# Attention and feed-forward network on one core: a planner's table of operation lengths and result delays is set anew

## The chip, the cores and the metric

The kernel runs on one core of a Trainium2 chip. The metric is the device time of one execution in microseconds (us); the median of several runs counts. A core has five instruction queues that are followed in order: TensorE (PE, matrix products; PEld is its loading of weights), VectorE (DVE), ScalarE (ACT), GpSimd (POOL) and SyncE (SP, which here issues every DMA). An instruction that waits holds up all that stand behind it in its queue.

## The reference

```python
scores = scale * np.matmul(q, k.transpose(0, 1, 3, 2))       # 8 batches x 8 heads, 576 x 576, depth 64
thresh = np.max(scores, axis=-1, keepdims=True) - tau
scores = np.where(scores >= thresh, scores, -1000000000.0)
attn = np.exp(scores - np.max(scores, axis=-1, keepdims=True))
attn = attn / (np.sum(attn, axis=-1, keepdims=True) + 1e-09)
x = np.matmul(attn, v)                                        # heads side by side: 4608 x 512
r = np.maximum(x @ w_in, 0.0)                                 # 512 x 2048
out = (s * (r * r) + b) @ w_out                               # 2048 x 512
```

`tau` is 0.02. `w_in` and `w_out` come as 64-bit floats, which the kernel turns into 32-bit floats itself.

## The kernel before, in words

**Attention.** A tile is 128 rows of queries of one head against all 576 keys. Batch 0 (36 tiles, "plain") is computed in 32-bit floats: scores on PE (L481), the row's maximum on DVE (L484), the exponential on ACT (L488), threshold and sum on DVE (L490), the division on POOL (L496), transposes on PE (L504), a copy on ACT (L508) and the product with the values on PE (L517). Batches 1 to 7 (252 tiles, "split") use pairs of 16-bit floats, a high and a low part of each number. Such a tile goes through scores on PE (L545, into bank `s` or `t`), maximum on DVE (L549), bias on ACT (L553) and the threshold on POOL (L551), exponential on ACT (L555), threshold and sum on DVE (L557), a small POOL instruction (L560), reciprocal on DVE (L562), high part on ACT (L563), low part on DVE (L566), and then a transposing DMA issued by SP (L571) into the tiles `ea` and `eb`. When the 4 or 5 tiles of a visit are there, PE multiplies them with the values (L581, 28 matmuls); there are 56 such groups. Since the first and the last link of this chain are on PE, it has to be covered by other PE work.

**Weights.** In the first hundred microseconds the 16 slices of `w_in` and the 16 of `w_out` are loaded (L601, L604) and converted: two ACT instructions (L625, L628) and one DVE instruction (L620) for a slice. Then their size is found (L643 to L667), and only after that ACT (L692) and DVE (L696) make the 16-bit pieces that the network's matmuls need.

**Feed-forward network.** The rows of `x` go through in 18 blocks of 256 rows, each in 16 steps, 288 steps in all. A step is 12 matmuls into bank `h` (L794), three ACT instructions (L798 reads `h`, L801 squares, L802 makes the high part `gh`), one on POOL for the low part `gl` (L803; on DVE in the last block), and two groups of three matmuls (L809: two with `gh`, one with `gl`) into bank `o`. Bank `h` counts as one, so the next step's matmuls have to wait until L798 has read it.

**What sets the order.** Nothing runs where the code calls it. Each call of `plan.add` only records an operation with its engine, its keys (what it reads and writes) and two numbers: how long it occupies its engine, and after how long its result is there. `Plan.run` adds to the second number a fixed time for the way to another engine (`HANDOVER`), and `Plan.place` fills every engine's queue with a list scheduler: of the operations whose inputs are there by these numbers, the most urgent goes next. It runs forward and backward four times and keeps the order whose planned end is earliest; then the instructions are issued in that order. On the chip the queues and semaphores alone decide when something runs, so the numbers act only through the order. 76 matmuls with no result (L933, "busy" fillers) stand in places of the first plain tiles.

Of the kernel before, what the change touches and what calls it, by code (L numbers as in the profile page):

```python
# [37 lines left out]
class Plan:  # L38
# [7 lines left out]
    HANDOVER = 150  # L46
# [70 lines left out]
    def run(self):  # L117
# [24 lines left out]
def tile_attention_ffn(ctx: ExitStack, tc: tile.TileContext, qT, kT, v, tau, w_in, w_out, s, b, out):  # L142


    nc = tc.nc
# [103 lines left out]
    def pe(n, cols, fn, r, w, at):  # L249

        plan.add("PE", (n * (0.417 * cols + 3), n * (0.417 * cols + 3) + 170), fn, r, w, at)
# [13 lines left out]
    def dma(kb, fn, r, w, at):  # L265
        plan.add("SP", (max(600, kb * 4.4), 1550 + kb * 4.4), fn, r, w, at)

    def load(kb, fn, r, w, at):
        plan.add("SP", (max(620, kb * 4.4), 1550 + kb * 4.4), fn, r, w, at)


    def transfer(rows, fn, r, w, at):
        plan.add("SP", (1640, 3190), fn, r, w, at)

    class Plain:
# [27 lines left out]
        def load(self, at):  # L303
# [18 lines left out]
            if self.p:  # L322
                act((1900, 2000), zeros, ["qt0", "qt1"], [(self.tag, "z")], at)
# [41 lines left out]
    class Visit:  # L365
# [31 lines left out]
        def prepare(self, at):  # L397
# [5 lines left out]
            for c, (t, keys) in enumerate([(t, [k]) for t, k in raw] + [(flat, kr)]):  # L403
                w = t.shape[-1]
                ks.append((f"vm{m}", c))
                dve((67 + 1.04 * w, 150 + 1.04 * w), lambda c=c, t=t: nc.vector.tensor_reduce(
# [16 lines left out]
            for c, (t, key) in enumerate(raw):  # L423
                up, hi, lo = x[:, 9 + c:10 + c], 1 - c, 2 + c
                act((612, 717), lambda hi=hi, t=t, up=up: nc.scalar.activation(
                    out=self.piece(hi), in_=t, func=AF.Copy, scale=up), [key, (kx, 3)], [self.kpc[hi]], at)
                dve2((658, 743), lambda hi=hi, lo=lo, t=t, up=up: nc.vector.scalar_tensor_tensor(
# [17 lines left out]
            for hd in self.hds:  # L445
# [4 lines left out]
                act((350, 453), lambda hd=hd, own=own, j=j, up=up: nc.scalar.activation(  # L450
                    out=hd.values()[:, :, own], in_=rv[:, j], func=AF.Copy, scale=up), kr + [(kx, 3)], keys, at)
                dve2((400, 485), lambda hd=hd, own=own, other=other, j=j, up=up: nc.vector.scalar_tensor_tensor(
# [15 lines left out]
    def plain_tile(ti, i):  # L468
# [13 lines left out]
        plan.add("PE", (990, 1160), scores, ti.kq(), [bk, ("begun", i)], i - SCORES_AHEAD)  # L482
# [7 lines left out]
        dve((740, 900), lambda: nc.vector.scalar_tensor_tensor(  # L490
# [5 lines left out]
        pool((740, 748), lambda: nc.gpsimd.tensor_scalar(  # L496
# [8 lines left out]
        pe(5, 240, transposes, [em_k, "ident"], ["t"], i + 0.5)  # L505
        ke = ("e32", ti.slot)

        act((690, 790), lambda: nc.scalar.copy(out=e32(ti.slot), in_=tp), ["t"], [ke], i + 0.5)  # L508
        if ti.plain:
# [9 lines left out]
            plan.add("PE", (8.5 * n + 240, 8.5 * n + 410), products, [("e32", slot) for slot, _ in cuts] + [(pr.tag, "z")] + pr.kept[1] + [  # L519
                k for x in pr.keys[2:] for k in (x, x + (1,))], ["pv"], i + VALUES_AFTER)  # L520
            act((80 + 0.75 * n, 180 + 0.75 * n), lambda: nc.scalar.copy(out=dest, in_=bank["pv"][:, 0:n]), ["pv"], keys,
                i + VALUES_AFTER)

    def split_tile(ti, i):
# [21 lines left out]
        plan.add("PE", (4 * 123 + (190 if ti.slot is None else 0), 4 * 123 + (360 if ti.slot is None else 170)), scores,  # L546
# [4 lines left out]
        pool((260, 263), lambda: nc.gpsimd.tensor_scalar(  # L551
            out=line, in0=top, scalar1=-1.0, scalar2=va.wz[:, 2:3], op0=ALU.mult, op1=ALU.add), [(ks_, 0), (va.kwz, 2)], [(ks_, 1)], i - 0.5)
# [4 lines left out]
        dve((740, 900), lambda: nc.vector.scalar_tensor_tensor(  # L557
# [5 lines left out]
        act((668, 774), lambda: nc.scalar.activation(out=pieces[:, 0:S], in_=ex, func=AF.Copy, scale=unit),  # L563
            [em_k, (ks_, 3)], [en_k], i)
        act((142, 242), lambda: nc.scalar.copy(out=pieces[:, S:S + T], in_=pieces[:, 0:T]), [en_k], [(en_k, 1)], i)
# [500 lines left out]
```

## Time and profile before

| | |
|---|---|
| median of 3 runs | 1137.09 us (1134.49 to 1138.08) |
| the profiled execution, its own time | 1137.64 us |
| its span, first to last instruction | 1135.8 us |
| PE busy | 1106.7 us (97%) |
| DVE, ACT, POOL busy | 917.3, 967.7, 546.5 us |
| DMA queues, share of 16 engines | 65% |
| granted TensorE clock | 1.00 of full speed in every slice |

Busy time is the union of an engine's instructions. The length that the profile gives for one instruction runs from start to end; on ACT and DVE the next one starts some 0.1 us before that end, so what an instruction takes of its engine is read from start to start.

### The profile page before, as it was taken

What the parts mean: (1) busy time and instruction counts of PE and PEld (TensorE: products, weight loads), DVE (VectorE), ACT (ScalarE), POOL (GpSimd) and SP (SyncE); (2) the same over time, 40 slices, a digit from 0 to 9 for tenths busy, and PEclk for the clock granted to TensorE, in tenths of its full rate; (3) what the DMA queues carried; (4) which work ended last, traced back from release to release, by engine and by line L of the source; (5) the groups of instructions that cost most, each with busy time, mean ns of one, the idle gap of its engine ahead of it and who ended that gap; (6) DMA issues with size and microseconds to landing.
All of it is one profiled execution on the core that took longest, in us unless ns stands there. A gap on an engine that the chain in (4) does not pass through costs nothing.

```text
span 1135.8 us, 26196 instructions
## 1 busy us (share of the span) xinstructions
PE 1106.7 (97%) x8882; PEld 770.5 (68%) x8882; DVE 917.3 (81%) x1950; ACT 967.7 (85%) x2301; POOL 546.5 (48%) x1117
## 2 busy tenths in 40 slices
PE   8998999999999999999999999999999999999998
PEld 7776656666676666766666667666666667666665
DVE  5898889898999998989789799988988898875021
ACT  7997889889999988999889799998889989896443
POOL 5665445455645554545435355554545555443200
PEclk9999999999999999999999999999999999999999
DMA  8940069777987987668757499777876777563000
GB/s 277 342 143 1 13 163 178 145 151 138 213 151 136 156 195 166 137 117 168 168 113 149 84 179 181 163 142 167 163 153 130 131 152 126 94 110 58 10 20 19
DMA packets 360438, 156.27 MB, mean 138 GB/s; under 512 B 314224, under 2 KB 342384, under 8 KB 360304
## 3 DMA queue, kind: packets, MB, share of 16 engines
q1 hardware_dynamic: 360304, 154.60, 65.1%
q8 instruction: 70, 1.15, 0.4%
q14 instruction: 64, 0.52, 0.2%
HBM read 46.01 MB, written 9.44 MB: 49 GB/s over the span
## 4 chain that ended last, share of the span: by engine, by line
PE 74%; ACT 8%; DVE 6%; issue 3%; DMA 3%; POOL 1%; SPq 1%; DVEq 0%; ACTq 0%; POOLq 0%
PE h L794 27%; PE o L809 27%; PE pv L581 7%; PE s L545 4%; PE t L545 4%; ACT en L563 2%; ACT em L555 1%; DVE em L557 1%; DMA eb<-en 1%; PE pv L517 1%; DVE st L549 1%; ACT iw L798 1%; DMA ea<-en 1%; PE t L504 1%; PE s L481 1%
## 5 line engine op out<-in xcount | busy, mean ns | idle before, releaser
L794 PE MATMUL h<-xp,iw 128*128 128x256 f16 x3456 | 424.8, 273 | 10.2 <-ACT iw L798 9.4
L794 PEld LDWEIGHTS <-iw 128*128 128x128 f16 x3456 | 335.2, 98 | 100.1 <-issue 20.5
L803 POOL TENSOR_TENSOR gl<-iw,gh 128x256 f16<-128x256 f32 x272 | 202.3, 744 | 208.4 <-issue 82.6
L566 DVE SCALAR_TENSOR_TENSOR en<-em,st,en 128x576 f16<-128x576 f32 x252 | 209.6, 836 | 21.4 <-ACT en L563 20.1
L563 ACT ACTIVATE en<-em,st 128x576 f16<-128x576 f32 x252 | 193.0, 768 | 17.0 <-DVE st L562 9.4
L809 PE MATMUL o<-ow,gh 128*128 128x512 f16 x648 | 192.9, 379 | 0.7 <-DVE iw L823 0.7
L551 POOL TENSOR_SCALAR st<-st,wz 128x1 f32<-128x1 f32 x252 | 121.5, 483 | 111.3 <-DVE st L549 68.0
L798 ACT ACTIVATE iw<-h 128x256 f32<-128x256 f32 x288 | 108.0, 375 | 71.2 <-PE h L794 62.8
L809 PEld LDWEIGHTS <-gh 128*128 128x128 f16 x1152 | 108.2, 98 | 77.7 <-issue 8.2
L560 POOL TENSOR_SCALAR st<-st 128x1 f32<-128x1 f32 x252 | 86.1, 342 | 144.1 <-DVE em L557 76.2
L809 PE MATMUL o<-iw,gh 128*128 128x512 f16 x504 | 150.0, 379 | 0.2 <-DVE iw L823 0.2
L809 PE MATMUL o<-ow,gl 128*128 128x512 f16 x324 | 122.8, 379 | 0.0
L801 ACT ACTIVATE iw<-iw 128x256 f32<-128x256 f32 x288 | 119.4, 415 | 3.7
L802 ACT CAST gh<-iw 128x256 f16<-128x256 f32 x288 | 115.5, 401 | 4.5 <-PE o L809 0.5
L557 DVE SCALAR_TENSOR_TENSOR em<-t,st,em 128x576 f32<-128x576 f32 x126 | 102.3, 812 | 19.9 <-ACT em L555 13.6
L545 PEld LDWEIGHTS <-ow 128*128 128x128 f16 (+1 forms) x980 | 85.1, 100 | 47.8 <-issue 13.5
L557 DVE SCALAR_TENSOR_TENSOR em<-s,st,em 128x576 f32<-128x576 f32 x126 | 102.3, 812 | 13.0 <-ACT em L555 8.9
L555 ACT ACTIVATE em<-s,st,wz 128x576 f32<-128x576 f32 x126 | 103.9, 824 | 1.1
L555 ACT ACTIVATE em<-t,st,wz 128x576 f32<-128x576 f32 x126 | 103.8, 824 | 1.1
L553 ACT ACTIVATE st<-st,wz 128x1 f32<-128x1 f32 x252 | 72.9, 290 | 36.3 <-DVE st L549 34.8
L809 PEld LDWEIGHTS <-gl 128*128 128x128 f16 x576 | 56.3, 98 | 68.0
L549 DVE TENSOR_REDUCE st<-t 128x1 f32<-128x576 f32 x126 | 94.4, 749 | 8.8 <-PE t L545 7.2
(198 smaller groups left out, 1836.1 us busy)
## 6 DMA issues: line engine op xcount, KB each, us to landing
ow<-k SPq DMA_DIRECT2D x98, 216.0 KB, 3.5
rk<-in_k_dram SPq DMA_DIRECT2D x29, 288.0 KB, 3.3
iw<-in_moe_w_in_dram SPq DMA_DIRECT2D x16, 512.0 KB, 6.8
ow<-in_moe_w_out_dram SPq DMA_DIRECT2D x16, 512.0 KB, 6.1
out_dram<-iw SPq DMA_DIRECT2D x32, 256.0 KB, 2.5
rq<-in_q_dram SPq DMA_DIRECT2D x28, 288.0 KB, 3.6
rv<-in_v_dram SPq DMA_DIRECT2D x56, 128.0 KB, 2.8
qs<-k SPq DMA_DIRECT2D x14, 216.0 KB, 3.6
```

The costliest lines, as they stand in the source:

```text
L545: nc.tensor.matmul(to, y[:, 0, q], y[:, w, c], start=(w == 1), stop=(w == 2))
L551: pool((260, 263), lambda: nc.gpsimd.tensor_scalar(out=line, in0=top, scalar1=-1.0, scalar2=va.wz[:, 2:3], op0=ALU.mult, op1=ALU.add), [(k ...
L555: act((636, 740), lambda: nc.scalar.activation(out=halves, in_=ps, func=AF.Exp, bias=bias, scale=va.wz[:, 1:2]), [bk, (ks_, 4), (va.kwz, 1 ...
L557: dve((740, 900), lambda: nc.vector.scalar_tensor_tensor(out=halves, in0=ps, scalar=line, in1=halves, op0=ALU.is_ge, op1=ALU.mult, accum_o ...
L563: act((668, 774), lambda: nc.scalar.activation(out=pieces[:, 0:S], in_=ex, func=AF.Copy, scale=unit), [em_k, (ks_, 3)], [en_k], i)
L566: dve2((740, 825), lambda: nc.vector.scalar_tensor_tensor(out=pieces[:, S + T:2 * S + T], in0=ex, scalar=unit, in1=pieces[:, 0:S], op0=ALU ...
L794: nc.tensor.matmul(ps, wi[w][f][:, c * P:(c + 1) * P], x[:, u, c, :], start=(c == 0 and i == 0), stop=(c == NC - 1 and i == 2))
L798: act((357, 473), lambda: nc.scalar.activation(out=g(), in_=ps, func=AF.Relu, scale=H_DOWN), [h, (f"w{SPARES[(0, 1, 5)[k3]]}", "i", 2)], [ ...
L801: act((320, 417), lambda: nc.scalar.activation(out=g(), in_=g(), func=AF.Square), [kg], [kg], at)
L802: act((308, 405), lambda: nc.scalar.copy(out=hi, in_=g()), [kg], [f"gh{k3}"], at)
L803: do((712, 735) if not self.last else (340, 425), lambda: eng.tensor_tensor(out=lo, in0=g(), in1=hi, op=ALU.subtract), [kg, f"gh{k3}"], [f ...
L809: nc.tensor.matmul(bank["o"][:, t, :], a[:, ts_], w, start=(f == 0 and i == 0), stop=(f == NF - 1 and i == 2))
```

## The change

The numbers given to `plan.add` are replaced, and the fixed time for the way to another engine becomes 40 ns, or 110 ns where the receiver is POOL, in place of 150 ns everywhere. No instruction is added, removed or altered; the counts of instructions on each engine are the same. The core of the diff (other lines of the same kind are left out):

```diff
-    HANDOVER = 150
+    HANDOVER, TO_POOL = 40, 110
...
-                lag = p[2] + self.HANDOVER if p[0] != o[0] else p[2] if p[0] != "PE" else p[1]
+                lag = p[2] + (self.TO_POOL if o[0] == "POOL" else self.HANDOVER) if p[0] != o[0] else p[2] if p[0] != "PE" else p[1]
...
     def load(kb, fn, r, w, at):
-        plan.add("SP", (max(620, kb * 4.4), 1550 + kb * 4.4), fn, r, w, at)
+        plan.add("SP", (max(660, kb * 3.5), 2000 + kb * 5), fn, r, w, at)
...
     def transfer(rows, fn, r, w, at):
-        plan.add("SP", (1640, 3190), fn, r, w, at)
+        plan.add("SP", (1450, 3400), fn, r, w, at)
...
-        act((636, 740), lambda: nc.scalar.activation(out=halves, in_=ps, func=AF.Exp, bias=top, scale=1.0),
+        act((633, 800), lambda: nc.scalar.activation(out=halves, in_=ps, func=AF.Exp, bias=top, scale=1.0),
...
-        pool((260, 263), lambda: nc.gpsimd.tensor_scalar(
+        pool((290, 255), lambda: nc.gpsimd.tensor_scalar(
             out=line, in0=top, scalar1=-1.0, scalar2=va.wz[:, 2:3], op0=ALU.mult, op1=ALU.add), [(ks_, 0), (va.kwz, 2)], [(ks_, 1)], i - 0.5)
-        act((100, 200), lambda: nc.scalar.activation(out=bias, in_=top, func=AF.Copy, scale=va.wz[:, 1:2]),
+        act((185, 300), lambda: nc.scalar.activation(out=bias, in_=top, func=AF.Copy, scale=va.wz[:, 1:2]),
             [(ks_, 0), (va.kwz, 1)], [(ks_, 4)], i - 0.5)
-        act((636, 740), lambda: nc.scalar.activation(out=halves, in_=ps, func=AF.Exp, bias=bias, scale=va.wz[:, 1:2]),
+        act((716, 885), lambda: nc.scalar.activation(out=halves, in_=ps, func=AF.Exp, bias=bias, scale=va.wz[:, 1:2]),
...
-            plan.add("PE", (12 * 0.427 * NB, 12 * 0.427 * NB + 170), products, self.kx + [(f"w{f}", "i", 2)], [h], at)
-            act((357, 473), lambda: nc.scalar.activation(out=g(), in_=ps, func=AF.Relu, scale=H_DOWN),
+            plan.add("PE", (12 * 0.4265 * NB, 12 * 0.4265 * NB + 220), products, self.kx + [(f"w{f}", "i", 2)], [h], at)
+            act((264, 400), lambda: nc.scalar.activation(out=g(), in_=ps, func=AF.Relu, scale=H_DOWN),
...
-            do((712, 735) if not self.last else (340, 425), lambda: eng.tensor_tensor(out=lo, in0=g(), in1=hi, op=ALU.subtract),
+            do((735, 735) if not self.last else (400, 490), lambda: eng.tensor_tensor(out=lo, in0=g(), in1=hi, op=ALU.subtract),
```

The first place is ACT's queue at the first plain tiles, from the first exponential on (`em` are the exponentials, `iw` and `ow` slices of the weights, `x` and `rv` the transposed tiles). Before:

```order
L488 ACTIVATE em_78<-s,st_69 128x576
L488 ACTIVATE em_79<-o,st_70 128x576
L488 ACTIVATE em_80<-s,st_71 128x576
L508 COPY x_113<-t 128x640
L488 ACTIVATE em_78<-o,st_72 128x576
L625 ACTIVATE iw_235<-iw_235 128x512
L508 COPY rv<-t 128x640
L628 ACTIVATE iw_235<-iw_235 128x512
```

After:

```order
L488 ACTIVATE em_78<-s,st_69 128x576
L625 ACTIVATE iw_187<-iw_187 128x512
L488 ACTIVATE em_79<-o,st_70 128x576
L628 ACTIVATE iw_187<-iw_187 128x512
L488 ACTIVATE em_80<-s,st_71 128x576
L508 COPY x_113<-t 128x640
L488 ACTIVATE em_78<-o,st_72 128x576
L625 ACTIVATE ow_221<-ow_221 128x512
```

The two conversions of the first slice have moved from behind the fourth exponential to behind the first and the second.

The second place is ACT's queue in the first block of the network, from the reading of bank `h` (L798) in step 13 on, where the first split tiles come in (`k` is a piece of a raw tile, `st` are row statistics, `gh` the high part). Before:

```order
L798 ACTIVATE iw_292<-h 128x256
L425 ACTIVATE k<-rq,vs_103 128x576
L553 ACTIVATE st_71<-st_71,wz_90 128x1
L801 ACTIVATE iw_292<-iw_292 128x256
L555 ACTIVATE em_80<-s,st_71,wz_90 128x576
L553 ACTIVATE st_72<-st_72,wz_90 128x1
L802 CAST gh_115<-iw_292 128x256
L555 ACTIVATE em_78<-t,st_72,wz_90 128x576
L798 ACTIVATE iw_325<-h 128x256
```

After:

```order
L798 ACTIVATE iw_236<-h 128x256
L801 ACTIVATE iw_236<-iw_236 128x256
L802 CAST gh_115<-iw_236 128x256
L798 ACTIVATE iw_285<-h 128x256
L801 ACTIVATE iw_285<-iw_285 128x256
L802 CAST gh_116<-iw_285 128x256
L798 ACTIVATE iw_333<-h 128x256
```

Two exponentials, two biases and a conversion of a raw tile no longer stand between the two readings of `h`; the first split tiles come later, behind 16 steps of the network where it was 12.

## Rows read from the trace of the kernel before

**Rows 1.** The profile's page: span, and each engine's busy time.
```profile
span 1135.8 us, 26196 instructions
PE 1106.7 (97%) x8882; PEld 770.5 (68%) x8882; DVE 917.3 (81%) x1950; ACT 967.7 (85%) x2301; POOL 546.5 (48%) x1117
```

**Rows 2.** Busy time of each engine by stretch of 50 us; then clock, DMA share, GB/s.
```profile
0.00:50.00 50.00, 45.81 (x341) 38.21 (x343) 35.60 (x84) 41.70 (x81) 30.20 (x81) 1.00 0.94 320
50.00:100.00 50.00, 46.20 (x454) 36.21 (x452) 44.61 (x104) 43.15 (x79) 30.07 (x57) 1.00 0.35 113
100.00:150.00 50.00, 47.38 (x381) 33.08 (x380) 38.95 (x72) 44.72 (x93) 26.56 (x44) 1.00 0.14 35
150.00:200.00 50.00, 46.01 (x349) 31.31 (x349) 45.65 (x100) 42.97 (x102) 24.87 (x52) 1.00 0.87 167
200.00:250.00 50.00, 47.31 (x401) 32.91 (x396) 45.50 (x97) 46.12 (x111) 24.84 (x51) 1.00 0.76 147
...
700.00:750.00 50.00, 50.00 (x411) 34.39 (x410) 45.94 (x98) 46.26 (x113) 25.15 (x53) 1.00 0.77 155
...
1100.00:1136.00 36.00, 31.45 (x211) 20.45 (x209) 6.51 (x14) 13.46 (x34) 0.00 (x0) 1.00 0.04 15
```

**Rows 3.** PE's waits in the whole run: us in total, times, longest.
```profile
PE h L794 <- ACT iw L798: 9.4, 9, 1.9
PE s L545 <- DVE em L557: 2.1, 2, 1.5
```

**Rows 4.** Timeline of PE, 155 to 163 us: start, length, instructions [idle before].
```profile
155.63 1.47 PE L794 MATMUL h<-xp,iw 128*128 128x256 f16 x12
158.98 1.47 PE L794 MATMUL h<-xp,iw 128*128 128x256 f16 x12 [1.88 <-ACT iw L798]
...
160.94 0.59 PE L809 MATMUL o<-iw,gh 128*128 128x512 f16 x2
...
161.59 1.47 PE L794 MATMUL h<-xp,iw 128*128 128x256 f16 x12
162.90 0.17 PE L411 MATMUL pv<-vm,onesb 128*128 128x4 bf16 x1
```

**Rows 5.** Timeline of ACT in the same stretch.
```profile
156.15 0.28 ACT L553 ACTIVATE st<-st,wz 128x1 f32<-128x1 f32 x1
...
156.64 0.81 ACT L555 ACTIVATE em<-s,st,wz 128x576 f32<-128x576 f32 x1
157.36 0.28 ACT L553 ACTIVATE st<-st,wz 128x1 f32<-128x1 f32 x1
...
158.56 0.37 ACT L798 ACTIVATE iw<-h 128x256 f32<-128x256 f32 x1
```

**Rows 6.** Timeline of ACT at the first plain tiles, and at 31 us.
```profile
10.62 0.74 ACT L488 ACTIVATE em<-o,st 128x576 f32<-128x576 f32 x1 [0.97 <-DVE st L484]
13.44 0.74 ACT L488 ACTIVATE em<-s,st 128x576 f32<-128x576 f32 x1 [2.08 <-DVE st L484]
...
30.92 0.67 ACT L625 ACTIVATE iw<-iw 128x512 f32<-128x512 f32 x1
31.48 0.68 ACT L628 ACTIVATE ow<-ow 128x512 int32<-128x512 uint16 x1
```

**Rows 7.** ACT's longest wait in 0 to 30 us: total, times, longest.
```profile
ACT em L488 <- DVE st L484: 5.3, 4, 2.1
```

**Rows 8.** As rows 2, around the network's first step.
```profile
100.00:105.00 5.00, 3.74 (x41) 3.00 (x40) 3.82 (x10) 4.70 (x8) 3.23 (x11) 1.00 0.01 2
105.00:110.00 5.00, 3.64 (x29) 3.15 (x29) 4.73 (x11) 5.00 (x12) 4.23 (x5) 1.00 0.01 3
```

**Rows 9.** The transposing DMAs of L571, all 280, from issue to landing.
```profile
DMA to landing us min/median/max: 2.8/3.4/7.0
```

**Rows 10.** POOL's threshold instruction L551: length in ns, min/median/max.
```profile
L551 POOL TENSOR_SCALAR st<-st,wz x252: 255/266/1402, 148.2 to 1025.7; 128x1 f32<-128x1 f32 x126
```

**Rows 11.** The page's group of DVE's low part L566: busy us, mean ns.
```profile
L566 DVE SCALAR_TENSOR_TENSOR en<-em,st,en 128x576 f16<-128x576 f32 x252 | 209.6, 836 | 21.4 <-ACT en L563 20.1
```

More of the change, by code (lines that the diff above doesn't have):

```diff
@@ L249, in pe @@
     def pe(n, cols, fn, r, w, at):
-        plan.add("PE", (n * (0.417 * cols + 3), n * (0.417 * cols + 3) + 170), fn, r, w, at)
+        plan.add("PE", (n * (0.417 * cols + 3), n * (0.417 * cols + 3) + 165), fn, r, w, at)
     def dve(cost, fn, r, w, at, port=False):
@@ L504, in transposes @@
                 nc.tensor.transpose(out=tp[:, t, :], in_=ex[:, c:c + P], identity=ident())
-        pe(5, 240, transposes, [em_k, "ident"], ["t"], i + 0.5)
+        plan.add("PE", (573, 816), transposes, [em_k, "ident"], ["t"], i + 0.5)
         ke = ("e32", ti.slot)
-        act((690, 790), lambda: nc.scalar.copy(out=e32(ti.slot), in_=tp), ["t"], [ke], i + 0.5)
+        act((572, 797), lambda: nc.scalar.copy(out=e32(ti.slot), in_=tp), ["t"], [ke], i + 0.5)
         if ti.plain:
@@ L518, in products @@
                                          e32(slot)[:, kt, cs], start=(kt == 0), stop=(kt == 4))
-            plan.add("PE", (8.5 * n + 240, 8.5 * n + 410), products, [("e32", slot) for slot, _ in cuts] + [(pr.tag, "z")] + pr.kept[1] + [
+            plan.add("PE", (8 * n + 220, 8 * n + 320), products, [("e32", slot) for slot, _ in cuts] + [(pr.tag, "z")] + pr.kept[1] + [
                 k for x in pr.keys[2:] for k in (x, x + (1,))], ["pv"], i + VALUES_AFTER)
-            act((80 + 0.75 * n, 180 + 0.75 * n), lambda: nc.scalar.copy(out=dest, in_=bank["pv"][:, 0:n]), ["pv"], keys,
+            act((50 + 0.83 * n, 150 + 0.83 * n), lambda: nc.scalar.copy(out=dest, in_=bank["pv"][:, 0:n]), ["pv"], keys,
                 i + VALUES_AFTER)
@@ L545, in scores @@
                         nc.tensor.matmul(to, y[:, 0, q], y[:, w, c], start=(w == 1), stop=(w == 2))
-        plan.add("PE", (4 * 123 + (190 if ti.slot is None else 0), 4 * 123 + (360 if ti.slot is None else 170)), scores,
+        plan.add("PE", (490 + (214 if ti.slot is None else 0), 650 + (126 if ti.slot is None else 0)), scores,
                  [("y", 2 * va.n + j, c) for j in js for c in range(2)], [bk], i - SCORES_AHEAD)
@@ L562, in split_tile @@
         dve((73, 157), lambda: nc.vector.reciprocal(out=unit, in_=total), [(ks_, 2)], [(ks_, 3)], i)
-        act((668, 774), lambda: nc.scalar.activation(out=pieces[:, 0:S], in_=ex, func=AF.Copy, scale=unit),
+        act((666, 760), lambda: nc.scalar.activation(out=pieces[:, 0:S], in_=ex, func=AF.Copy, scale=unit),
             [em_k, (ks_, 3)], [en_k], i)
-        act((142, 242), lambda: nc.scalar.copy(out=pieces[:, S:S + T], in_=pieces[:, 0:T]), [en_k], [(en_k, 1)], i)
-        dve2((740, 825), lambda: nc.vector.scalar_tensor_tensor(
+        act((135, 225), lambda: nc.scalar.copy(out=pieces[:, S:S + T], in_=pieces[:, 0:T]), [en_k], [(en_k, 1)], i)
+        dve2((728, 830), lambda: nc.vector.scalar_tensor_tensor(
             out=pieces[:, S + T:2 * S + T], in0=ex, scalar=unit, in1=pieces[:, 0:S], op0=ALU.mult, op1=ALU.subtract),
@@ L582, in products @@
                                      lazy[("ea", "eb")[j]][:, n, g.c0:g.c0 + g.n], start=(i == 0), stop=(i == len(slots) - 1))
-        cost = len(slots) * (0.417 * g.n + 3) + 150
-        plan.add("PE", (cost, cost + 170), products, g.keys + [k for hd in g.hds for k in hd.kvs], ["pv"], at)
+        cost = len(slots) * (0.417 * g.n + 3) + 206
+        plan.add("PE", (cost, cost + 85), products, g.keys + [k for hd in g.hds for k in hd.kvs], ["pv"], at)
         hd = g.hds[0]
@@ L724, in sums @@
         hs = ["h"]
-        plan.add("PE", (8 * 216, 8 * 216 + 170), products, [(f"w{f}", "o", 2) for f in fs] + ["ones16"], hs, at)
+        plan.add("PE", (8 * 216, 8 * 216 + 160), products, [(f"w{f}", "o", 2) for f in fs] + ["ones16"], hs, at)
         if k == 0:
@@ L728, in sums @@
         else:
-            dve((660, 745), lambda: nc.vector.tensor_tensor(out=spare(2), in0=bank["h"], in1=spare(2), op=ALU.add),
+            dve((600, 680), lambda: nc.vector.tensor_tensor(out=spare(2), in0=bank["h"], in1=spare(2), op=ALU.add),
                 hs + ["bias"], ["bias"], at)
@@ L755, in stage @@
             for u, c in enumerate(self.cuts):
-                dve((100 + 4.2 * size[u], 190 + 4.2 * size[u]), lambda u=u, c=c: nc.vector.tensor_reduce(
+                dve((63 + 4.17 * size[u], 143 + 4.17 * size[u]), lambda u=u, c=c: nc.vector.tensor_reduce(
                     out=nm[:, u:u + 1], in_=self.src[:, :, c], axis=mybir.AxisListType.XY, op=ALU.max,
@@ L773, in stage @@
                 up = pw[:, 2, u:u + 1]
-                act((110 + 3.64 * size[u], 212 + 3.64 * size[u]), lambda c=c, up=up: nc.scalar.activation(
+                act((185 + 3.34 * size[u], 285 + 3.34 * size[u]), lambda c=c, up=up: nc.scalar.activation(
                     out=get()[:, 0, :, c], in_=self.src[:, :, c], func=AF.Copy, scale=up),
@@ L777, in stage @@
                     [kx, (kx, 0), (kx, 1)] + [(kx, h, v) for h in range(2) for v in range(4)] if not u else [(kx, 0, u)], at)
-                dve2((130 + 4.18 * size[u], 230 + 4.18 * size[u]), lambda c=c, up=up: nc.vector.scalar_tensor_tensor(
+                dve2((135 + 4.15 * size[u], 225 + 4.15 * size[u]), lambda c=c, up=up: nc.vector.scalar_tensor_tensor(
                     out=get()[:, 1, :, c], in0=self.src[:, :, c], scalar=up, in1=get()[:, 0, :, c], op0=ALU.mult,
```

38 lines of the change are left out of this document (19 added, 19 removed).

## Prediction

> **What bounds the kernel now.** I read the page first: PE is busy for 1106.7 of 1135.8 us [rows 1]. The reader should take two things from it. The same matmuls are issued before and after, so the change can only move the time that PE is not at work, some 29 us, and whatever useless waiting hides inside its busy time. And the other engines have room on average, so they matter only where PE waits for them.
>
> The table by stretches [rows 2] says where the 29 us lie. PE lacks 4.2, 3.8, 2.6, 4.0 and 2.7 us in the first five stretches of 50 us, 17.3 us together. At 700 us it lacks nothing in 50. At the very end it lacks 4.6, which is the last result's way out. So the first 250 us and the end hold 22 of the 29 us; the some 850 us between them hold about 7. The granted clock is 1.00 throughout and is no part of the question.
>
> Then the waits of PE [rows 3]. The largest has one cause: the next step's matmuls (L794) wait until ACT has read bank `h` (L798), 9.4 us in 9 places, the longest 1.9. The next largest is 2.1. The rest of the idle time is start, end and short gaps.
>
> Last the timeline at the longest of these waits [rows 4, 5]. A step occupies PE for 1.31 us (161.59 to 162.90). Here the next step stands directly behind one that began at 155.63, and starts only at 158.98. ACT is why: it was working through biases and exponentials, and came to L798 at 158.56. One such exponential takes ACT 157.36 − 156.64 = 0.72, and a bias (L553) lasts 0.28 from start to end. The old table has 0.636 for the first and lets the second's result be there after 0.200; the new one has 0.716 and 0.300. So the old plan believed that ACT would be through earlier than it can be, and the order that it made puts PE in front of a door that is still shut.
>
> **The change, part by part.** No instruction is added or removed, so each term is a wait that moves.
>
> *Steps that stand close together.* I counted in the two orders how much PE work lies between one step's matmuls and the next's, with 0.65 us for a group of L809 [rows 4] and about 0.5 for a split score tile. Before, 11 places have at most one such group or tile between them, in five of them nothing at all; after, it is 8, in two of them nothing and in one a single small matmul. The 9.4 us lie nearly all at these places [rows 3], 0.85 us for each of the 11. Eight of them at that price are 6.8 us: a gain of 2.6 us. The bounds: with ACT's lengths right, all eight could be free of waits, a gain of 9.4; or each could cost the longest wait, 1.9, which is 15.2 in all and a loss of 5.8. I take the middle price, since the places that stay are of the same kind, the first one again in the first block.
>
> *The start.* In the first 30 us ACT waits four times, 5.3 us together, for the maximum of a plain tile [rows 7]. Into two of these waits (0.97 and 2.08) the new order puts the first slice's two conversions [rows 6], 0.56 us each (30.92 to 31.48). That is 1.1 us that ACT needn't spend later. The whole of the conversions moves forward: the first L692, which needs all of them, stands behind 32 exponentials and 30 copies of plain tiles before, behind 29 and 27 after. So the network's first step should come some 4 to 5 us earlier (six instructions at about the 0.6 that a conversion takes, and the 1.1). This is not a gain of that size: the three tiles' work is still to be done, and PE has then done about as much less by that time. I cost the shift itself at nothing, since ACT is busy 42 to 45 us of each 50 in that part [rows 2] and what it does first it doesn't do later; the cover is the plain tiles left over, which now lie beside the first steps, where PE stands idle for 2.6 us of 10 [rows 8]. If they cover that too, 2.6 more are gained; if the weights land too late for their new places, each late slice stops ACT and the plain tiles behind it, and I allow 4 us of loss for that, half of the 8.0 us that PE lacks in the first 100 us [rows 2]. I take the 1.1 us.
>
> *The way between engines.* 150 ns become 40 (110 to POOL). A split tile's chain from PE to PE goes over nine such ways, one of them to POOL, so the plan brings the last link nearer to the first: up to 8 × 0.11 + 0.04 = 0.92 us, of which the longer table entries (for the transposing DMA 3.40 in place of 3.19) take back a part. Where PE always has other work this is worth nothing, and at 700 us it has [rows 2]: I cost it at nothing. What hides it is PE work between the last score tile of a visit and the product with the values; that cover shrinks, see the first rival.
>
> *SP's queue.* The table allows a transposing DMA 1.45 us of the queue in place of 1.64, and loads come in another order. All were covered (PE's waits show no DMA of weight [rows 3]): nothing.
>
> The sum is −2.6 − 1.1 = −3.7 us on the profiled execution's 1137.6. That execution lies 0.5 above the median of the three runs, 1137.1, which gives **1133.4 us**, 0.33% less. A measurement of this kernel can tell about 0.3%, 3.4 us, from no change, so the forecast lies at that border.
>
> **The rivals.**
>
> *No change to be seen.* PE is full for most of the run; the 17 us of the first stretches come from a start-up that is a chain (load, convert, find the size, make pieces), and the short filler places are only traded for others of the same price. For it: 97% [rows 1]. Against it: the waits for L798 have a cause that the new table mends [rows 5]. Time 1137.
>
> *The ramp gains more.* With true lengths the stretches from 50 to 250 us, which lack 13.1 us, could come halfway to the 0 of the later ones [rows 2]: 6.5 us in place of the 3.7, and the end stays as it is. With 2.6 from the later steps' waits it is 9.1, so 1128. For it: these stretches are where ACT is fullest and wrong lengths hurt most. Against it: the first split tiles stand behind 16 steps where it was 12, so the attention chain comes in later and its first product too.
>
> *Slower: the product with the values waits for its transposes.* Counted in the order by PE's work, the least distance from a visit's last score tile to its product (L581) falls from 11.6 to 9.5 us, and 7 of the 56 visits lie under 12 us where it was 2. The transposing DMAs land after 3.4 us as a rule, but after 7.0 at the worst [rows 9], and the new plan reckons with 3.4 and a handover of 0.04. A DMA that is late by 3.6 then stops PE, and everything in its queue. If each of the seven loses a third of that, 1.2, the loss is 8.4, and with the 3.7 gained the time is 1141.8. It decides from 7.1 us of such waits on, since up to there the time stays within 0.3% of the old one. For it: the distance that shrinks. Against it: of PE's long waits none was of this kind [rows 3], so there was slack to give.
>
> *Slower: POOL's lengths don't hold.* The table gives the threshold instruction one length, 0.255 to its result. The row shows a median of 0.266 and a longest of 1.402 [rows 10], 1.14 more; a DVE instruction of L566 has 0.836 [rows 11]. In some 20 steps the low part's product now stands 2.6 to 2.8 us behind the step's matmuls by PE's work, where it was 3.2 to 3.4; each needs POOL's `gl`. If POOL is late by half of 1.14 in all of these, and nothing covers it, it costs 20 × 0.57 = 11.4, less the 3.7: 1144.8; with half of them covered, 1139.1. The Trainium skill has the rule for such lateness (SBUF — State Buffer, section "SBUF: two separate sides"): DVE and GpSimd share a port pair as an exclusive lock, and whoever comes second waits for the other's whole instruction. The long tail of the row agrees with it; the rule speaks against a fixed length for POOL, though the planner keeps one such port for both engines, before and after.
>
> **How the numbers follow.** The forecast (1131 to 1136) gets 0.40, no change 0.24, the ramp 0.16, the transposes 0.13, POOL 0.07. The border to "faster" is 1133.7: of the forecast's 0.40 some 0.24 lie below it, with the ramp's 0.16 that is 0.40. The other 0.16 of the forecast, nearly all of the no-change case and a part of POOL's make 0.40 for the same. The transposes, the rest of POOL and a start whose weights come late make 0.20 for slower. The range has to take in the ramp at its best (1128 less some 2) and the transposes (1141.8): 1126 to 1142.
>
> **What the profile would show.** If I am right, PE's waits for L798 fall from 9.4 us to about 7, with fewer of them in the first block; ACT's wait for the maxima in the first 30 us falls by about a microsecond; the first step of the network starts at 97 to 100 us; and no wait of PE on a transposing DMA appears. The forecast is wrong if PE's idle time in the stretches after 250 us grows above the 7 us of before (then the handovers were slack that was needed), or if the first 250 us lack clearly more or less than 17 us.

## The result, and the profile after

The changed kernel took **1148.3 us** (median of 4 runs, 1146.8 to 1151.5), the kernel before 1137.2 beside it: 1.0105 of the time, with an interval of 1.0077 to 1.0133. It is 1% slower, and lies above the range that the prediction gave. The page of the changed kernel, its lines that answer to [rows 1]:

```profile
span 1147.2 us, 26153 instructions
PE 1111.1 (97%) x8882; PEld 770.8 (67%) x8882; DVE 917.4 (80%) x1950; ACT 967.0 (84%) x2301; POOL 538.3 (47%) x1117
```

The span grew by 11.4 us. PE's busy time is 4.4 longer and its idle time 7.0 (1147.2 − 1111.1 = 36.1, where it was 29.1). The table by stretches, with the columns of [rows 2], shows where; first of the kernel after:

```profile
0.00:50.00 50.00, 43.40 (x346) 36.87 (x347) 35.78 (x85) 42.91 (x84) 27.67 (x77) 1.00 0.95 320
50.00:100.00 50.00, 47.28 (x449) 37.04 (x448) 46.65 (x106) 44.91 (x83) 33.55 (x67) 1.00 0.33 113
100.00:150.00 50.00, 49.94 (x393) 34.41 (x392) 36.70 (x68) 40.84 (x87) 25.80 (x38) 1.00 0.03 8
150.00:200.00 50.00, 46.73 (x347) 31.21 (x347) 42.86 (x93) 42.27 (x101) 24.37 (x50) 1.00 0.84 197
200.00:250.00 50.00, 47.75 (x398) 32.35 (x395) 48.72 (x108) 47.29 (x116) 26.10 (x54) 1.00 0.74 138
250.00:600.00 350.00, 344.73 (x2797) 236.96 (x2796) 316.22 (x675) 315.32 (x773) 178.55 (x366) 1.00 0.79 159
600.00:1050.00 450.00, 439.92 (x3545) 301.35 (x3543) 372.24 (x780) 389.26 (x956) 208.32 (x441) 1.00 0.71 134
```

The two long stretches of the kernel before:

```profile
250.00:600.00 350.00, 344.73 (x2806) 237.13 (x2805) 315.77 (x675) 314.66 (x773) 178.96 (x364) 1.00 0.76 154
600.00:1050.00 450.00, 448.38 (x3621) 307.97 (x3619) 379.39 (x801) 397.33 (x975) 219.74 (x453) 1.00 0.71 137
```

In the first 250 us PE lacks 14.9 us where it lacked 17.3: the start did gain 2.4. From 250 to 600 its idle time is the same. From 600 to 1050 PE lacks 10.1 where it lacked 1.6, a loss of 8.5; and the way out at the end lacks about 1 more. PE's waits between 600 and 1050 us (total, times, longest) show what is new there. After:

```profile
PE pv L581 <- DMA eb<-en: 3.3, 5, 1.1
PE h L794 <- ACT iw L798: 1.7, 4, 0.6
PE t L545 <- DVE em L557: 1.6, 3, 0.8
PE s L545 <- DVE em L557: 1.5, 1, 1.5
PE pv L581 <- DMA ea<-en: 0.8, 1, 0.8
PE pv L704 <- ACT x L588: 0.4, 1, 0.4
```

Before, the same stretch held 1.3 us of waits in all, none of them longer than 0.4 and none on a DMA:

```profile
PE o L809 <- DVE iw L823: 0.7, 2, 0.4
PE h L794 <- DVE xp L778: 0.2, 1, 0.2
PE h L794 <- ACT iw L798: 0.2, 1, 0.2
PE h L794 <- ACT xp L774: 0.2, 1, 0.2
```

Now products wait for their transposes (4.1 us, six times), scores for a bank, steps for ACT. Over the whole run `h` waits 5.2 us for L798 (9.4 in [rows 3]), L581 4.9 us for the transposing DMAs (none before), and L545 6.9 us (2.8 before), of which 4.6 are for DVE and 2.3 for the copies of `k`. So PE's matmuls wait 7.2 us for SP's transposes and copies, where before they did not wait for them at all. The other waits nearly balance: those for ACT fell from 15.3 us to 8.1, those for DVE rose from 5.5 to 12.9.

One of these places, followed back. SP's queue from 946 us on: start, time in the queue, instruction (L434 are copies of 216 KB, pieces of `k` into the operands of the split scores; x3 are three of them).

```profile
946.00 1.29 SPq L571 DMA_TRANSPOSE eb<-en  x1
947.39 2.88 SPq L434 DMA_DIRECT2D ow<-k  x3
950.37 1.58 SPq L571 DMA_TRANSPOSE ea<-en  x1
952.06 1.67 SPq L571 DMA_TRANSPOSE eb<-en  x1
```

The chain of work at the same place, and PE's timeline:

```profile
951.93 0.13 issue
952.06 3.80 DMA eb<-en
955.86 0.04 issue
955.90 1.14 PE pv L581 x17
```

```profile
953.01 1.47 PE L794 MATMUL h<-xp,iw 128*128 128x256 f16 x12
954.49 0.27 PE L581 MATMUL pv<-ea,ow 128*64 128x256 f16 x1
955.90 0.27 PE L581 MATMUL pv<-eb,ow 128*64 128x256 f16 x1 [1.15 <-DMA eb<-en]
```

The queue has no gap longer than 0.11 us, and the DMA engines are at work 0.74 to 1.00 of each 4 us around it (all 16, by the table of stretches from 938 to 956 us; 0.74 and 0.89 in the two that hold these six transfers). From 946.00 the three transposes and three copies hold the queue until 953.73: 7.73 us. The new table books 3 × 1.45 + 3 × 0.756 = 6.62 for them (216 KB at 3.5 ns are 0.756 us), the old one 3 × 1.64 + 3 × 0.950 = 7.77. So the last transpose was issued 0.9 us later than the new entries add up to (952.06 − 946.00 = 6.06 against 5.17), took 3.80 in place of 3.40 to land, and PE stood for 1.15.

### The profile page after: what moved, and what is told of

Same layout as the page of the kernel before. It is cut to its first block, busy times and chain, and to the rows that moved or that the text cites. A ratio compares the mean times of both kernels' runs of the same rounds, so it can differ in the third digit from the quotient of the medians.

```text
span 1147.2 us, 26153 instructions
## 1 busy us (share of the span) xinstructions
PE 1111.1 (97%) x8882; PEld 770.8 (67%) x8882; DVE 917.4 (80%) x1950; ACT 967.0 (84%) x2301; POOL 538.3 (47%) x1117
## 3 DMA queue, kind: packets, MB, share of 16 engines
q8 instruction: 70, 1.15, 0.4%
## 4 chain that ended last, share of the span: by engine, by line
PE 63%; ACT 13%; DVE 9%; DMA 7%; issue 6%; SPq 1%; POOL 1%; DVEq 0%; ACTq 0%; POOLq 0%
PE o L809 23%; PE h L794 22%; PE pv L581 6%; PE t L545 4%; PE s L545 3%; DMA eb<-en 3%; DVE em L557 2%; ACT en L563 2%; ACT em L555 2%; DVE st L549 2%; ACT iw L798 1%; DVE en L566 1%; DMA rv<-in_v_dram 1%; PE pv L517 1%; DMA ow<-k 1%
## 5 line engine op out<-in xcount | busy, mean ns | idle before, releaser
L794 PE MATMUL h<-xp,iw 128*128 128x256 f16 x3456 | 425.2, 273 | 9.1 <-ACT iw L798 5.2
L794 PEld LDWEIGHTS <-iw 128*128 128x128 f16 x3456 | 334.8, 98 | 97.0 <-issue 20.2
L803 POOL TENSOR_TENSOR gl<-iw,gh 128x256 f16<-128x256 f32 x272 | 196.2, 721 | 204.5 <-issue 85.0
L566 DVE SCALAR_TENSOR_TENSOR en<-em,st,en 128x576 f16<-128x576 f32 x252 | 208.6, 830 | 29.0 <-ACT en L563 27.1
L563 ACT ACTIVATE en<-em,st 128x576 f16<-128x576 f32 x252 | 193.3, 770 | 19.3 <-DVE st L562 11.4
L551 POOL TENSOR_SCALAR st<-st,wz 128x1 f32<-128x1 f32 x252 | 126.9, 504 | 117.4 <-DVE st L549 77.2
L798 ACT ACTIVATE iw<-h 128x256 f32<-128x256 f32 x288 | 108.5, 377 | 71.9 <-PE h L794 67.0
L560 POOL TENSOR_SCALAR st<-st 128x1 f32<-128x1 f32 x252 | 81.7, 324 | 158.3 <-DVE em L557 105.7
L545 PEld LDWEIGHTS <-ow 128*128 128x128 f16 (+1 forms) x980 | 85.0, 100 | 54.9 <-issue 18.2
L549 DVE TENSOR_REDUCE st<-s 128x1 f32<-128x576 f32 x126 | 94.6, 751 | 10.0 <-PE s L545 9.5
```

The lines of the kernel that those rows point to most:

```text
L545: nc.tensor.matmul(to, y[:, 0, q], y[:, w, c], start=(w == 1), stop=(w == 2))
L549: dve((667, 750), lambda: nc.vector.tensor_reduce(out=top, in_=ps, axis=mybir.AxisListType.XY, op=ALU.max, negate=True), [bk], [(ks_, 0)], ...
L551: pool((290, 255), lambda: nc.gpsimd.tensor_scalar(out=line, in0=top, scalar1=-1.0, scalar2=va.wz[:, 2:3], op0=ALU.mult, op1=ALU.add), [(k ...
L563: act((666, 760), lambda: nc.scalar.activation(out=pieces[:, 0:S], in_=ex, func=AF.Copy, scale=unit), [em_k, (ks_, 3)], [en_k], i)
L566: dve2((728, 830), lambda: nc.vector.scalar_tensor_tensor(out=pieces[:, S + T:2 * S + T], in0=ex, scalar=unit, in1=pieces[:, 0:S], op0=ALU ...
L794: nc.tensor.matmul(ps, wi[w][f][:, c * P:(c + 1) * P], x[:, u, c, :], start=(c == 0 and i == 0), stop=(c == NC - 1 and i == 2))
```

## What the DMA engines spend

I added up, in the trace of the kernel before, the time that packets of one kind took, as a share of 16 engines, and compared it with what the table books for SP's queue. The transposes are the only great source of 256-byte packets (286,720 of 298,496); the copies of L434 are the packets of 3456 and 1152 bytes.

```
                    engines' time      each            new table  old table
280 transposes      434 to 452 us      1.55 to 1.61    1.45       1.64
112 copies, 216 KB  109.1 us           0.974           0.756      0.950
```

SP's queue mostly goes on sooner than that. The transposes' times in the queue, after (ns, shortest/median/longest):

```profile
L571 SPq DMA_TRANSPOSE ea<-en x140: 1200/1300/3279, 166.2 to 1041.9; - x140
...
DMA to landing us min/median/max: 2.8/3.4/6.2
```

So the median of the queue's interval, 1.30, is less than a transpose costs the engines; at the place above the intervals were 1.58 and 1.67. What lengthens an interval is not settled: over all 280, sorted by how busy the engines were in the 3 us before, the median stays between 1.27 and 1.31. The landing hardly differs from [rows 9], and 3.4 as a delay is right in the middle.

Summed over all its transfers, the table books 824 us of SP's queue before and 729 after; the DMA queues' share on the page, 65.7% of 16 engines before, is 746 us, of which 739 are SP's. By this sum the new table looks nearly right, but it hides two errors. For transposes and copies the old table books 566 us and the new one 491, where 543 to 561 are spent; all other transfers are booked at 238 by the new one and spend 178 to 196. The new table is short for the two kinds that the attention chain waits for, and long for the rest.

## The experiments

All ratios are to the kernel before on the same chip, with the 95% interval. Three theories stood at first: S, that the short ways between engines (40 and 110 ns) took away slack that was needed; L, that the new lengths of the engines' operations are wrong; and D, that any change of the table draws another order, and orders differ by chance. SP's bookings came as a fourth.

**e1_ways_only.** The kernel before with only the new ways.

```diff
-    HANDOVER = 150
+    HANDOVER, TO_POOL = 40, 110
```

> The kernel before with one edit: the way between engines is 40 ns (110 to POOL) in place of 150, all lengths as before. Theory S (slack): the 110 ns of every way were cover that the chip's in-order queues need; most of the 11 us lost come from here, so 1144 to 1149, with PE's waits spread over 600 to 1050 us. Theory L (lengths): the loss comes from the new lengths of operations; then this is 1134 to 1139. Theory D (draw): any change of the table draws another order, and orders that the planner holds for equal differ by up to 1% on the chip; then it can be anywhere in 1130 to 1150 and its waits have other causes than those of the changed kernel.

1142.4 us, 1.0060 [1.0043, 1.0077]: about half of the loss, beside the old lengths, and between what S and L had said.

**e2_ways_back.** The new table with the old ways.

```diff
-    HANDOVER, TO_POOL = 40, 110
+    HANDOVER, TO_POOL = 150, 150
```

> The changed kernel with the ways put back to 150 ns everywhere, all new lengths kept. Theory S: 1135 to 1140, the waits on transposes in 600 to 1050 us are gone. Theory L: 1145 to 1150. Theory D: anywhere in 1130 to 1150. By the order's counts this one has steps whose second product stands 1.8 us behind its first (2.3 in the changed kernel), so two or three waits of about 1 us are expected in any case.

1146.6 us, 1.0095 [1.0074, 1.0116]: the loss stays, against S. But this run is no clean reading, since TensorE's clock fell in it for 13.7 us (last section), which is worth some 6 us. e3 decides.

**e3_sp_back.** The changed kernel with SP's three old entries; all else of the new table stays.

```diff
-        plan.add("SP", (max(600, kb * 3.5), 2000 + kb * 5), fn, r, w, at)
+        plan.add("SP", (max(600, kb * 4.4), 1550 + kb * 4.4), fn, r, w, at)
...
-        plan.add("SP", (1450, 3400), fn, r, w, at)
+        plan.add("SP", (1640, 3190), fn, r, w, at)
```

> The changed kernel with SP's entries put back (loads 1.55 us + 4.4 ns per KB, a transpose 1.64 us of the queue and 3.19 to its result). Theory S: the planned result of a transpose comes 0.21 us earlier still, so no better than the changed kernel: 1146 to 1152. Theory that the denser planning of SP's queue (1.45 us for a transpose) is the cause: 1137 to 1141. Theory D: anywhere in 1130 to 1150.

1135.3 us, 0.9999 [0.9988, 1.0010]: the whole loss is gone with three lines. S and L both fall as the cause by themselves, as the short ways and PE's, ACT's, DVE's and POOL's new lengths are all in it.

**e4_near_before.** How much does the time move when the table says nearly the same? The kernel before with 145 for 150.

```diff
-    HANDOVER = 150
+    HANDOVER = 145
```

> The kernel before with the way between engines at 145 ns in place of 150 and nothing else: a table that is as right or wrong as the old one, but gives another order. Theories S and L: 1134 to 1141, like the kernel before within 0.3%. Theory D: more than 0.3% away, on either side; the kernel before was then the best of many draws, and a part of the 11 us is only that the new table was drawn once.

1138.2 us, 1.0027 [1.0017, 1.0036]. Another order of the same table is worth 0.3%; a difference of that size between two tables proves nothing.

**e5_transpose_back** and **e6_loads_back.** The changed kernel, with only the transposes' old entry (e5) or only the old entries of copies and loads (e6), as in the diff of e3.

> The changed kernel with one entry put back: a transposing DMA takes 1.64 us of SP's queue and 3.19 to its result (1.45 and 3.40 in the changed one). With all of SP's entries put back the time was 1135.3, that of the kernel before. Theory Q (the transposes are planned too close on SP's queue): this alone gives 1134 to 1139. Theory M (the entries of plain loads and copies, 3.5 ns per KB of the queue in place of 4.4, are the cause): 1143 to 1149. Theory D (draws of orders): neither, anything in 1133 to 1149.

> The changed kernel with the entries of plain loads and copies put back (4.4 ns per KB of the queue, 1.55 us + 4.4 ns per KB to the result), the transposes' entry kept at 1.45 and 3.40. Theory Q: 1143 to 1149. Theory M: 1134 to 1139. Theory D: anything in 1133 to 1149.

e5: 1142.2 us, 1.0070 [1.0052, 1.0088]; e6: 1143.3 us, 1.0080 [1.0064, 1.0096]. Each alone takes back less than half of the loss, and both together (e3) take back all. How much either is worth can't be said closer, since these steps of 0.3% are no larger than e4's.

**e7_transpose_cover.** Is it the products alone that wait? The transposes' result is booked 0.6 us later, the queue as in the changed kernel.

```diff
-        plan.add("SP", (1450, 3400), fn, r, w, at)
+        plan.add("SP", (1450, 4000), fn, r, w, at)
```

> The changed kernel with one entry altered: a transposing DMA's result is planned after 4.00 us in place of 3.40, its queue time stays at 1.45. If the loss is the products' waiting on transposes that land late (my first rival), 0.6 us of cover takes these waits away: PE's 4.9 us on transposing DMAs fall to under 1, and the time to 1135 to 1141. If the queue time of 1.45 is what hurts, the waits move to other places and the time stays at 1143 to 1149.

1142.0 us, 1.0068 [1.0052, 1.0084]. L581 waits 0.5 us for its transposes in place of 4.9, but by the ratios only about a third of the loss comes back. PE's waits (total, times, longest) show what is left:

```profile
PE h L794 <- ACT iw L798: 6.1, 13, 1.3
PE s L545 <- DMA ow<-k: 3.4, 4, 1.4
...
PE s L545 <- DVE em L557: 2.2, 6, 0.8
...
PE t L545 <- DMA ow<-k: 1.1, 2, 0.6
```

The copies go through the same queue and come late as before; now the scores wait 4.5 us for them, where it was 2.3.

**e8_sp_only.** The counterpart of e3: the kernel before with SP's three new entries and nothing else.

> The kernel before with SP's new entries alone (loads, copies and transposes), everything else old. If SP's entries are the cause by themselves: 1143 to 1149. If they hurt only together with the short ways between engines, which leave no cover: 1134 to 1140. Theory D: anything in 1133 to 1149. By the order's counts one visit's product stands 6.6 us behind its last score tile here (9.5 at the least in the changed kernel), which costs some 2 to 4 us in any case.

1150.0 us, 1.0134 [1.0116, 1.0152]: SP's entries alone make a loss at least as large. Its place and its kind are others, though. From 600 to 1050 us PE lacks only 3.4 us here, but 20.7 in the first 250, and the clock fell there (the last column but two is the granted clock):

```profile
0.00:250.00 250.00, 229.32 (x1849) 167.25 (x1851) 201.34 (x437) 210.84 (x445) 136.03 (x276) 0.97 0.55 150
```

Of all PE's waits only 2.0 us are for transposes and copies, and 15.7 are for DVE. So this run shows that the entries cost time, but not that they do it by late transfers alone.

**e9_dma_time.** If the entries should say what the DMA engines spend, the changed kernel with the transposes at 1.64 and the copies at 4.4 ns for a KB (0.95) should lose nothing; delays and loads stay new. It books 805 us.

```diff
-        plan.add("SP", (max(600, kb * 3.5), 2000 + kb * 5), fn, r, w, at)
+        plan.add("SP", (max(600, kb * 4.4), 2000 + kb * 5), fn, r, w, at)
...
-        plan.add("SP", (1450, 3400), fn, r, w, at)
+        plan.add("SP", (1640, 3400), fn, r, w, at)
```

> The changed kernel with two entries altered: a transposing DMA books 1.64 us of the queue (1.45 in the changed one), plain copies 4.4 ns per KB (3.5), their results after 3.40 us and 2 us + 5 ns per KB as in the changed one; loads stay at 3.5. Theory B (booking): the new table books less of the DMA engines' time than the transfers take, so the plan sets transfers closer than they can run; with the booking back this is 1134 to 1140. If it is the results' delays that matter (3.40, 2.0 + 5 ns per KB), the time stays at 1142 to 1150. Theory D (draws of orders): anything in 1134 to 1150.

**1129.2 us, 0.9952 [0.9936, 0.9968]**: faster than both kernels, and than the 1134 to 1140 expected. Its page, its long stretches, and all its waits of PE from 600 to 1050 us that are longer than 0.3:

```profile
span 1127.4 us, 26145 instructions
PE 1104.7 (98%) x8882; PEld 770.4 (68%) x8882; DVE 918.6 (81%) x1950; ACT 963.2 (85%) x2301; POOL 543.9 (48%) x1117
```

```profile
250.00:600.00 350.00, 347.86 (x2841) 240.22 (x2841) 321.87 (x689) 318.54 (x786) 183.69 (x375) 1.00 0.80 159
600.00:1050.00 450.00, 447.16 (x3589) 306.64 (x3586) 371.41 (x781) 391.44 (x960) 209.62 (x442) 1.00 0.69 132
```

```profile
PE pv L411 <- DVE vm L406: 0.8, 1, 0.8
PE o L809 <- POOL gl L803: 0.6, 1, 0.6
PE o L809 <- DVE iw L823: 0.6, 1, 0.6
```

No product waits for a transpose there and no score for a copy. PE lacks 2.1 us from 250 to 600, where both kernels lack 5.3, and 2.8 from 600 to 1050.

**e10_sp_less.** The dose in the other direction: transposes at 1.30, the median of SP's interval, copies and loads at 2.6 ns. It books 645 us.

> The changed kernel with still less booked: 1.30 us of the queue for a transposing DMA (the median interval at which SP issues it in the profile), 2.6 ns per KB for loads and copies, results as in the changed one. Theory B: slower than the changed kernel, 1149 to 1158. If the queue times don't matter: 1142 to 1150. Theory D: anything in 1134 to 1150.

1166.9 us, 1.0292 [1.0262, 1.0321], above even the 1149 to 1158 expected. The same waits as after, twice as long:

```profile
PE h L794 <- ACT iw L798: 10.0, 19, 2.0
PE pv L581 <- DMA eb<-en: 9.3, 9, 1.8
PE s L545 <- DVE em L557: 4.0, 5, 1.2
```

**e11_near_after** and **e12_near_before2.** Neighbours again: the changed kernel with ways of 45 and 115, the kernel before with 155.

> The changed kernel with the ways between engines at 45 and 115 ns in place of 40 and 110 and nothing else: a table as good as the new one, but another order. Theory B: still slow, 1142 to 1150. Theory D: it can be anywhere in 1134 to 1150. The distance from 1148 is the size of what one draw is worth. By the order's counts three steps have their second product less than 2 us behind the first one's end, which costs some 2 us in any case.

> The kernel before with the ways at 155 ns in place of 150 and nothing else, another order from a table as good as the old one. Theory B: 1134 to 1141. Theory D: anything in 1134 to 1150. By the order's counts three scores stand less than 2.5 us behind the last use of their bank (none in the kernel before), which costs some 2 us each in any case.

e11: 1148.0 us, 1.0124 [1.0104, 1.0144], so the loss is not one order's bad luck. e12: 1141.8 us, 1.0065 [1.0049, 1.0081], just above what theory B allowed: the old table's neighbours are up to 0.65% slower than it, and 150 is a good draw of that table. In e12 a part of that is the clock again, which fell for 10.2 us. e1's 0.6% can be no more than a draw.

**e13_sp_more.** Is more booking always better? e9 with the transposes at 1.85, copies at 5.3 and loads at 4.4 ns, 911 us in all.

> The kernel of e9 (1129.2) with more booked than the transfers take: 1.85 us of the queue for a transposing DMA, 5.3 ns per KB for copies, 4.4 for loads, results as there. Theory B with the DMA engines' time as the measure: booking more buys nothing and makes the plan hold back transfers that could run, 1128 to 1138. If any cover on SP's queue is good: faster than e9 again, 1120 to 1127. Theory D: anything in 1128 to 1145.

1138.6 us, 1.0021 [1.0010, 1.0033]: the gain is lost again. That there is an optimum between is not shown by it: the clock fell here for 10.2 us at 226 us, behind waits of scores for DVE, which is worth some 5 of the 8 us (0.7%) that lie between e13 and e9:

```profile
0.00:250.00 250.00, 234.06 (x1905) 172.15 (x1906) 209.08 (x450) 216.52 (x461) 138.98 (x282) 0.98 0.57 155
```

**e14_near_e9** and **e15_e9_ways_150.** e9 with ways of 45 and 115, and with the old 150 for all.

> The kernel of e9 with the ways between engines at 45 and 115 ns in place of 40 and 110 and nothing else: another order from an equally good table. Theory B: on the fast side of the kernels that book too little, 1127 to 1138. Theory D: anything in 1128 to 1150. By the order's counts it has ten steps with at most one short group between them where e9 has five, which costs some 3 us.

> The kernel of e9 with the ways between engines put back to 150 ns everywhere. Theory S (the ways' cover is needed): faster than e9, 1122 to 1128. If the cover isn't needed once SP's bookings are right: 1128 to 1138.

e14: 1129.6 us, 0.9940 [0.9924, 0.9955]: the gain holds in a second order. e15: 1135.5 us, 0.9993 [0.9982, 1.0003]: some 5 us slower with the long ways, which is no more than one draw can be.

All together, by what the table books for SP's queue, in all and for transposes and copies alone (the engines spend 739 and 543 to 561 us). The waits are PE's, in us, for transposes and copies over the whole run. A star marks runs in which the clock fell in the middle.

```
booked us     ratio to the kernel before, and the waits for transposes and copies
645   (431)   1.0292 and 10.6 (e10)
729   (491)   1.0105 and 7.2 (after), 1.0124 and 9.3 (e11*), 1.0095 and 4.8 (e2*), 1.0134 and 2.0 (e8*)
              1.0068 and 5.0 (e7, with the delay at 4.0)
771   (512)   1.0080 and 3.8 (e6*)
782   (544)   1.0070 and 6.4 (e5*)
805   (566)   0.9952 and 0.3 (e9), 0.9940 and 0.5 (e14), 0.9993 and 1.6 (e15, ways of 150)
824   (566)   1 and 0 (before), 0.9999 and 3.0 (e3*), 1.0027 and 2.6 (e4), 1.0065 and 0.3 (e12*), 1.0060 and 0.4 (e1)
911   (646)   1.0021 and 0.8 (e13*)
```

Every table with the new entries for both kinds lies above every table with the old queue times for both, e7 above e12 only by a hair. That is the finding. Single steps inside a row are draws, and with the clock's share taken off (some 6 us in e2, 2 to 6 in the other starred runs) e2 would fall among the slower tables of 824. The two ends, e10 against e9 and e14, are free of that doubt, and e3 loses nothing in spite of its star.

## Why the prediction was wrong

**SP's queue is the step that failed.** It said of the transposes at 1.45 in place of 1.64: all were covered, nothing. The cover was read from [rows 3], and there it was in part the old table's doing: by booking 566 us for the 543 to 561 that transposes and copies spend, it left them room to land before PE came. With 491 booked, the plan gives them less than the engines spend on them, and sets work behind them that starts late: products by their transposes, scores by copies, 7.2 us of waits where there were none. e3 and e8 show from both sides that SP's entries make the loss; e10 and e9 show that it goes by the dose. The sign that the prediction had named came too: PE's idle time between 250 and 1100 us grew from 7.4 to 16.3 us. But the reading that it gave in brackets, that the handovers were needed slack, is not the cause, since e3 keeps them short and loses nothing. I priced only the change of the entry (0.19 us, hidden), not that an entry also decides how closely the planner packs. It should have been set beside the DMA engines' time per transfer, which the trace of before held all along: 1.55 to 1.61 us a transpose, 0.974 a copy. The Trainium skill (DMA: Bandwidth & Descriptors, section "Latency and other measured facts") gives 261 GB/s, measured on one kernel, for a transposing DMA with a non-contiguous middle dimension; for 1024 packets of 256 bytes that is 1.00 us as an estimate, and by it even 1.30 would have been ample. The trace and e10 say otherwise, and they decide.

**The rival of the late transposes** had the place right and part of the size: 4.9 us of waits in seven places where it had 8.4 in seven; that the two sevens are the same places is not shown. Its reason, less distance and a handover of 0.04, holds for these waits only: with SP's new entries the products wait 4.9 and 3.4 us behind ways of 40 and 45 (after, e11), but 0.5 behind ways of 150 (e2, e8). So they need the short ways and the short entries together. They are not the whole loss: in e2 and e7 these waits are down to 0.5 us, and the kernels stay slow, with 4.3 and 4.5 us of waits for copies from the same queue.

**Steps that stand close together** went as foretold in the sum: 5.2 us, the longest 0.8, where 6.8 were forecast and [rows 3] had 9.4. The two factors were off both ways, which is luck: 12 places waited where 8 were counted, and each cost 0.43, not 0.85. Why the price fell is not shown. Orders from the old lengths pay 0.41 to 1.04 us a place (e8, before), orders from the new ones 0.40 to 0.63 (e5, e14), so 0.85 was read from one order.

**The start** gained 2.4 us in the first 250 where 1.1 was counted, and not in the way I had it. The first step came at 95.16 us, 8 us earlier, where 97 to 100 was forecast. ACT's longest waits in the first 30 us:

```profile
ACT em L488 <- DVE st L484: 3.6, 2, 3.1
ACT iw L625 <- DMA iw<-in_moe_w_in_dram: 1.9, 1, 1.9
```

Against [rows 7] the waits for maxima fell by 1.7, and a wait for a slice of the weights took their place: the conversion was put where its load had not landed yet. ACT won nothing there, and PE lacks 6.6 us in the first 50 where it lacked 4.2; the gain lies behind that, above all between 100 and 150 us, where PE lacks 0.06 in place of 2.6.

**The ways between engines** were costed at nothing. No run speaks clearly against that: e2 and after differ by 0.1%, but the clock is in e2; the 0.6% of e1 and the 0.4 to 0.5% between e15 and e9 or e14 are no more than one draw. Where the short ways do show is in the products' waits, above.

**POOL's lengths** were no matter: L551's mean rose from 483 to 504 ns, and no wait of PE for `gl` is among those of the changed kernel.

Were the other terms right, then? e3 is the whole change without SP's entries, and the forecast 0.33% is not in it (0.9999, no lower than 0.9988), though its steps wait only 3.8 us for L798 and its first 250 us lack only 13.7. Other waits took the place, 3.0 us for transposes and copies among them. e9 and e14, with two of SP's entries mended, are 0.5% and 0.6% faster than before, clear of the noise, but a draw can be worth as much. So the forecast gain is seen in two orders and missing in a third.

The 4.4 us of longer busy time are probably the ends of matmuls. A step's matmuls last 1.47 us from start to end, and what follows can start after 1.31 [rows 4], so wherever PE has to stand, some 0.16 us of it is counted as busy. In the trace PE stands still at 68 places after and at 45 before: 23 × 0.16 = 3.7 us, an estimate.

What stays open: what makes PE's waits for DVE differ from order to order (5.5 us before, 12.9 after, 15.7 in e8, but 13.2 in e12 with the old entries too); whether the best booking is just what the two kinds spend (e9 books 566 for 543 to 561, and no value between it and e13's 646 was tried); and how much of e1's 0.6% is more than a draw.

## What to carry to other kernels

Give a planner's transfer the time that it occupies the DMA engines (its packets' time as a share of 16 engines), not the interval at which the queue lets the next one go; and compare what the table books with what the trace says the engines spend, kind by kind, before trusting "no wait on a DMA": the sums, 729 and 739, would have hidden it here. An entry that is too short costs even where its own wait was never seen, because the order closes up around it. Judge a table by two or three neighbours of itself, since one order of a table is worth up to 0.65% here, and look at the granted clock of each before its time is read as the table's.

## What was not expected of the hardware

The granted clock of TensorE can fall in the middle of such a kernel. In e2 PE waited 3.09 us for a bank at 230 us, with only four matmuls in 4.5 us; the table of stretches (columns of [rows 2]) and PE's timeline:

```profile
230.00:234.50 4.50, 0.65 (x4) 0.39 (x4) 4.50 (x12) 4.50 (x9) 3.19 (x7) 1.00 0.50 120
234.50:241.50 7.00, 6.14 (x38) 3.80 (x39) 6.92 (x14) 5.76 (x14) 2.37 (x4) 0.53 0.71 142
```

```profile
233.05 0.65 PE L545 MATMUL s<-ow 128*128 128x288 f16 x4 [3.09 <-DVE em L557]
...
236.38 2.50 PE L794 MATMUL h<-xp,iw 128*128 128x256 f16 x11 [0.84 <-DVE xp L778]
```

After that wait the granted clock is 0.53 for 7 us, nearly the lower level (1.2 of 2.4 GHz): 11 matmuls of L794 take 2.50 us, where 12 take 1.47 in [rows 4]. So here PE's wait is paid a second time, by the work behind it, at about 1.9 times its usual length. In the changed kernel itself the clock stayed at 1.00 until its last microseconds, also behind a wait of 2.90 us at 14 us, and it is no part of its loss.

It is a part of other runs' times, in every one of them behind waits of PE. By the trace the granted clock was at 0.50 in the middle of the run for 13.7 us in e2 and in e8, 10.2 in e12 and in e13, 6.8 in e5, and 3.4 in e3, e6 and e11; in the kernel before and in e1, e4, e7, e9, e10, e14 and e15 it never was. At 1.9 times the usual length that costs at most some 6, 5, 3 and 2 us, an estimate, where PE would have been at work throughout. So orders with equal tables differ by their clock as well as by their waits.
